# A list scheduler's second pass: urgencies taken from deadlines in a linear-attention and mixture-of-experts kernel

## The chip, the cores and the metric

The kernel runs on one core of a Trainium2 chip. The metric is the device time of one execution in microseconds (us), the median of several executions. Engines are named as the profile names them: PE is TensorE's matmul, PEld its weight load, DVE is VectorE, ACT is ScalarE, POOL is GpSimd, and SP is SyncE, which only issues DMAs here.

## The reference

Two stages follow each other. Linear attention: phi is applied to q and k, keys and values are summed into a small matrix for each head, and queries read it with a normalisation. Then four dense experts, each with two layers, weighted by given probabilities.

```python
def _attn_ref(q, k, v):                      # q, k, v: (8, 8, 576, 64)
    def phi(x):
        return np.where(x > 0, x, np.exp(x) - 1.0) + 1.0
    q_p, k_p = (phi(q), phi(k))
    kv = np.einsum('bhsd,bhse->bhde', k_p, v)
    z = np.sum(k_p, axis=2)
    num = np.einsum('bhsd,bhde->bhse', q_p, kv)
    den = np.einsum('bhsd,bhd->bhs', q_p, z)[..., None] + 1e-06
    return (num / den).astype(np.float32)

def _moe_ref(x, domain_probs, w1, w2):       # x: (4608, 512), 4 experts, 512 -> 1024 -> 512
    p = domain_probs / (domain_probs.sum(-1, keepdims=True) + 1e-09)
    for e in range(E):
        h = np.maximum(x @ w1[e], 0.0)
        out += p[:, e:e + 1] * (h @ w2[e])
```

## The kernel before

The kernel writes no order by hand. Every piece of work is an operation of a planner (class `Plan`): `pl.add` records its engine, an assumed duration, an urgency `pri` (smaller is earlier), the function that emits its instructions, and what it reads and writes. Dependencies follow from these names. A DMA also has `lead` and `move`, the time before and during its movement; all movements share one assumed mover, and landing takes another 0.6 us before time 80 and 2.5 us after. A result used on another engine comes 0.28 us later (`HOP`), on the same engine 0.03.

`Plan.order` then lays all operations out in time. At each step it takes the engine that can start something first and, among the operations ready there within 0.1 us (`NEAR`), the one with the smallest urgency. POOL is an exception: its operations keep the order in which they were recorded. The operations are emitted in the order of the starts found, and each engine executes its own in that order.

The work falls into three parts.

- Start, to about 84 us. Batch 0's attention is computed pair of heads by pair (`attention`, `turn_x`), its rest rows by `rest_maps` and `rest_late`. POOL loads the weights and most of the inputs of batches 0 and 1. Batch 0 goes through the experts in plain products (`first_l1`, lines L594 and L626; `first_l2`, L604 and L661), with batch 1's attention between them. DVE forms sums of weights (`sums_w1` L546, `sums_w2` L567).
- The main stage, 64 units (block of rows, half, expert). A unit's times hang on `U(n) = 84 + 6.4 n`. `prep` scales x by the probabilities on ACT (xp, L706, urgency U-7) and transposes it by DMA from SP (xT, L708, three buffers). `xsums` forms differences of xT on DVE (xs, L724). `l1_seven` has seven products of 8 matmuls on three PSUM banks (L746), each followed by an ACT copy or relu (L763, L760) or a DVE fused relu (L766). Product 5 and product 7 of a unit write the same bank, with the relu between them. `ssums` forms differences of the hidden values on DVE (s4, L808), and `l2_unit` the seven products of the second layer (L822), interleaved with the next unit's first layer. After every fourth unit DVE adds up the output (L893 to L900) and SP stores it. The last unit has its own ending (L861, L888), with two stores from SP and two from ACT.
- Beside the units runs the attention of batches 2 to 7, a pair for every two units, from a hand-set time t on: loads from SP (L232), exp on ACT (ek, L412, urgencies t and t+1.5), phi on DVE (kqp, L404 and L405, t+1.5 and t+3), the values cast on ACT (vp, L408), the query's transpose from SP (qT, L443, t+4.5; in the first two batches on PE, L424 and L437), the key-value product on PE (kv, L457 and L460, t+6), its copy (kvz, L470), two products (nd, L481, t+7.5 and t+9) and two normalisations on DVE (L495, L497, t+8.25 and t+9.75).

A first-layer product at step i of unit n has urgency U(n)+0.9i, a second-layer one U(n+1)+0.45+0.9i.

Of the kernel before, what the change touches and what calls it, by code (L numbers as in the profile page):

```python
# [17 lines left out]
BIG = 3.0e38  # L18


class Plan:
# [3 lines left out]

    HOP = 0.28
    NEAR = 0.1

    def __init__(self):
# [4 lines left out]
    def add(self, eng, dur, pri, fn, r=(), w=(), move=0.0, after=0.0, lead=1.2):  # L36
# [15 lines left out]
        )  # L52
        return n

    def order(self):
        ops = self.ops
        left = [len(o["deps"]) for o in ops]
        users = [[] for _ in ops]
        for n, o in enumerate(ops):
            for d in o["deps"]:  # L60
                users[d].append(n)
        free = {o["eng"]: 0.0 for o in ops}
        ready = {e: {} for e in free}
        fixed = {"POOL": [n for n, o in enumerate(ops) if o["eng"] == "POOL"]}
        at = [o["after"] for o in ops]
        mover = 0.0

        def release(n):
            ready[ops[n]["eng"]][n] = at[n]

        for n in range(len(ops)):
            if left[n] == 0:
                release(n)
        start = [0.0] * len(ops)
        for _ in ops:
            best = None
            for e, cand in ready.items():
                if e in fixed:
                    cand = {n: cand[n] for n in fixed[e][:1] if n in cand}
                if not cand:  # L80
                    continue
                t = max(free[e], min(cand.values()))
                if best is None or t < best[0]:
                    best = (t, e, cand)
            t, e, cand = best
            n = min(
                (n for n, x in cand.items() if x <= t + self.NEAR),
                key=lambda n: (ops[n]["pri"], n),
            )
            o = ops[n]  # L90
            del ready[e][n]
            if e in fixed:
                fixed[e].pop(0)
            start[n] = max(t, at[n])
            free[e] = done = start[n] + o["dur"]
            if o["move"]:
                mover = max(done + o["lead"], mover) + o["move"]
                done = mover + (0.6 if mover < 80 else 2.5)
            o["start"], o["done"] = start[n], done
            for u in users[n]:  # L100
                lat = self.HOP if ops[u]["eng"] != e or o["move"] else 0.03
                at[u] = max(at[u], done + lat)
                left[u] -= 1
                if left[u] == 0:
                    release(u)
        return [ops[n] for n in sorted(range(len(ops)), key=lambda n: (start[n], n))]
# [932 lines left out]
```

## Time and profile before

| | us |
|---|---|
| median of 7 executions | 502.12 |
| lowest and highest | 501.82 and 504.18 |
| the profiled execution, its own time | 502.12 |
| its span in the profile | 500.4 |
| PE busy | 481.4 |
| DVE busy | 410.1 |
| ACT busy | 368.1 |
| POOL busy | 42.6 |
| HBM read and written | 45.16 and 9.44 MB |

The span is what the profile covers; about 1.7 us of the execution's time lie around it. A busy share is an average over parts of the program with different limits, so the stretches of the span are read one by one: first the landing of loads and the first pairs, then batch 0 in the experts, then the units, then the end. The number after L in the profile is a line of the kernel above. A group's name such as `l1b<-xs,w` is the tile written and the tiles read.

### The profile page before, as it was taken

What the parts mean: (1) busy time and instruction counts of PE and PEld (TensorE: products, weight loads), DVE (VectorE), ACT (ScalarE), POOL (GpSimd) and SP (SyncE); (2) the same over time, 40 slices, a digit from 0 to 9 for tenths busy, and PEclk for the clock granted to TensorE, in tenths of its full rate; (3) what the DMA queues carried; (4) which work ended last, traced back from release to release, by engine and by line L of the source; (5) the groups of instructions that cost most, each with busy time, mean ns of one, the idle gap of its engine ahead of it and who ended that gap; (6) DMA issues with size and microseconds to landing.
All of it is one profiled execution on the core that took longest, in us unless ns stands there. A gap on an engine that the chain in (4) does not pass through costs nothing.

```text
span 500.4 us, 14836 instructions
## 1 busy us (share of the span) xinstructions
PE 481.4 (96%) x6008; PEld 424.2 (85%) x6008; DVE 410.1 (82%) x1036; ACT 368.1 (74%) x694; POOL 42.6 (9%) x68
## 2 busy tenths in 40 slices
PE   2799999999999999999999999999999999999995
PEld 1444546999999999999999999999999999999994
DVE  6788997889998999798998898899988676767664
ACT  5737667987987798869886888788866767676541
POOL 8856400000000000000000000000000000000000
PEclk9999999999999999999999999999999999999999
DMA  8999947935777577465467674757632232323311
GB/s 242 233 236 231 263 107 167 262 74 159 145 159 161 127 150 157 114 185 138 128 117 176 116 182 117 139 144 148 153 61 78 52 86 45 86 44 85 45 44 44
DMA packets 124006, 67.51 MB, mean 135 GB/s; under 512 B 94480, under 2 KB 117776, under 8 KB 123936
## 3 DMA queue, kind: packets, MB, share of 16 engines
q1 hardware_dynamic: 115056, 51.53, 45.7%
q0 software_dynamic: 8720, 14.76, 13.8%
q8 instruction: 47, 0.77, 0.6%
q10 hardware_dynamic: 160, 0.26, 0.1%
q14 instruction: 23, 0.19, 0.1%
HBM read 45.16 MB, written 9.44 MB: 109 GB/s over the span
## 4 chain that ended last, share of the span: by engine, by line
PE 90%; DMA 3%; ACT 2%; DVE 2%; issue 1%; POOL 1%; DVEq 0%; POOLq 0%; ACTq 0%
PE l1b L746 38%; PE l2b L822 38%; PE l2b L604 5%; PE l1b L594 5%; DMA w<-in_moe_w_dram 2%; PE at L481 2%; PE at L457 1%; DMA vs<-in_v_dram 1%; ACT xp L706 1%; DVE ot L661 1%; ACT h L760 0%; DVE ot L888 0%; POOL kq L232 0%; PE at L460 0%; ACT p L763 0%
## 5 line engine op out<-in xcount | busy, mean ns | idle before, releaser
L746 PEld LDWEIGHTS <-w 128*128 128x128 f16 x2048 | 132.5, 98 | 4.7
L760 ACT ACTIVATE h<-l1b 128x512 f16<-128x512 f32 x128 | 76.8, 600 | 53.8 <-PE l1b L746 52.2
L822 PE MATMUL l2b<-w,h 128*128 128x256 f16 x768 | 114.9, 273 | 0.1
L822 PE MATMUL l2b<-t,s 128*128 128x256 f16 x768 | 112.6, 273 | 0.0
L746 PEld LDWEIGHTS <-w1x 128*128 128x128 f16 x1536 | 100.0, 98 | 5.0 <-issue 1.5
L822 PEld LDWEIGHTS <-s 128*128 128x128 f16 x1024 | 92.3, 98 | 7.3
L766 DVE CUSTOM_DVE_ANT_0 h<-l1b,p 128x512 f16<-128x512 f32 x64 | 44.1, 690 | 44.9 <-PE l1b L746 40.5
L746 PE MATMUL l1b<-xs,w1x 128*128 128x128 f16 x1024 | 78.0, 219 | 0.5 <-ACT l1b L763 0.3
L746 PE MATMUL l1b<-xT,w 128*128 128x128 f16 x1024 | 78.1, 219 | 0.0
L746 PE MATMUL l1b<-xs,w 128*128 128x128 f16 x1024 | 78.0, 219 | 0.0
L706 ACT ACTIVATE xp<-x,p_nat 128x512 f16<-128x512 f16 x112 | 76.3, 720 | 1.4 <-DMA xT<-xp 0.6
L822 PEld LDWEIGHTS <-h 128*128 128x128 f16 x768 | 67.4, 98 | 5.1 <-ACT h L760 0.4
L808 DVE TENSOR_TENSOR s<-h 128x512 f16<-128x512 f16 x128 | 53.8, 420 | 1.4
L763 ACT COPY u<-l1b 128x512 f32<-128x512 f32 x64 | 37.5, 585 | 12.5 <-PE l1b L746 12.2
L766 DVE CUSTOM_DVE_ANT_0 h<-l1b,u 128x512 f16<-128x512 f32 x64 | 43.8, 684 | 3.5 <-PE l1b L746 2.2
L763 ACT COPY l1b<-l1b 128x512 f32<-128x512 f32 x64 | 36.6, 572 | 13.1 <-PE l1b L746 11.8
L763 ACT COPY p<-l1b 128x512 f32<-128x512 f32 x64 | 37.5, 585 | 8.8 <-PE l1b L746 7.6
L724 DVE TENSOR_TENSOR xs<-xT,xs 128x256 f16<-128x256 f16 x128 | 36.9, 288 | 4.1 <-PE l1b L746 0.5
L412 ACT ACTIVATE ek<-kq 128x512 f16<-128x512 f32 x60 | 37.8, 631 | 2.1 <-DMA kq<-in_k_dram 1.7
L746 PE MATMUL l1b<-xT,w1x 128*128 128x128 f16 x512 | 39.0, 219 | 0.1
L822 PE MATMUL l2b<-w,s 128*128 128x256 f16 x256 | 38.4, 273 | 0.0
L405 DVE TENSOR_TENSOR kqp<-ek,kqp 128x512 f16<-128x512 f16 x64 | 27.2, 425 | 10.0 <-ACT ek L412 6.5
(114 smaller groups left out, 562.3 us busy)
## 6 DMA issues: line engine op xcount, KB each, us to landing
w<-in_moe_w_dram POOLq DMA_DIRECT2D x32, 256.0 KB, 7.2
out_dram<-ot SPq DMA_DIRECT2D x16, 512.0 KB, 3.1
kq<-in_k_dram SPq DMA_DIRECT2D x25, 256.0 KB, 3.1
vs<-in_v_dram SPq DMA_DIRECT2D x25, 256.0 KB, 3.3
kq<-in_q_dram SPq DMA_DIRECT2D x25, 256.0 KB, 4.0
kq<-in_k_dram POOLq DMA_DIRECT2D x5, 256.0 KB, 8.1
vs<-in_v_dram POOLq DMA_DIRECT2D x5, 256.0 KB, 7.6
kq<-in_q_dram POOLq DMA_DIRECT2D x5, 256.0 KB, 7.0
```

Source lines behind the costliest of these rows:

```text
L405: nc.vector.tensor_tensor(out=o, in0=ek[:, i], in1=o, op=AO.min)
L412: pl.add("ACT", 0.55, pri + i * step, lambda i=i: nc.scalar.activation(ek[:, i], kq[:, i], AF.Exp), r=(sk[i],), w=(("ek", ei, i),))
L594: nc.tensor.matmul(out=bank, lhsT=w1_sb[e][:, dc, fj * P : (fj + 1) * P], rhs=xt0[:, dc, :], start=(dc == 0), stop=(dc == DC - 1),)
L604: nc.tensor.matmul(out=bank, lhsT=hts[ht[fj]][:, c * P : (c + 1) * P], rhs=w2_sb[e][:, fj, :], start=(fj == 0), stop=(fj == FC - 1),)
L706: pl.add("ACT", 0.6, pri, lambda c=c, src=src, ps=ps: nc.scalar.activation(xp[:, c, :], src, AF.Copy, scale=ps), r=r, w=(("xp", xi, c),))
L724: lambda o=o, a=a, b_=b_: tt(out=o, in0=a, in1=b_, op=AO.subtract),
L746: nc.tensor.matmul(out=bank[:, fc * P : (fc + 1) * P], lhsT=wt[:, kc, fc * P : (fc + 1) * P], rhs=r[:, kc, :], start=(start and fc == 0 an ...
L760: return lambda: nc.scalar.activation(o, bank, AF.Relu)
L763: return lambda: nc.scalar.copy(o, bank)
L766: return lambda: nc.vector._custom_dve(TENSOR_ADD_SAT, out=o, in0=bank, in1=t, s0=BIG, s1=0.0)
L808: pl.add("DVE", 0.36, U(n + 1) + d - 0.5, lambda i=i, a=a, b_=b_, alu=alu: tt(out=s4[:, i], in0=a, in1=b_, op=alu), r=r, w=(Q(i),))
L822: nc.tensor.matmul(out=l2b[bank][:, half * HD : (half + 1) * HD], lhsT=a[:, c, :], rhs=w[:, c], start=(opens and first and c == 0), stop=( ...
```

## The change

`order` is renamed to `lay_out`, and a new `order` runs it twice. Between the two passes `deadlines` goes backward through all operations. A PE operation's deadline is its start in the first pass; every other one's is the earliest of its users' deadlines, less the delay to that user and its own duration; for a DMA also less `lead`, `move` and a landing time of 0.6 us, whatever the time. An operation that no PE operation depends on keeps the value BIG. These deadlines replace the urgencies of all operations that are not on PE; those on PE keep the hand-set ones. The second pass starts afresh with them, and its order is emitted. The landing time in the layout itself is now written as LAND, with 1.9 us added from time 80 on.

```diff
     HOP = 0.28
+    LAND = 0.6
     NEAR = 0.1
...
+    def deadlines(self):
+        ops = self.ops
+        late = [o["start"] if o["eng"] == "PE" else BIG for o in ops]
+        for n in range(len(ops) - 1, -1, -1):
+            o = ops[n]
+            for d in o["deps"]:
+                x = ops[d]
+                lat = self.HOP if x["eng"] != o["eng"] or x["move"] else 0.03
+                if x["move"]:
+                    lat += x["lead"] + x["move"] + self.LAND
+                late[d] = min(late[d], late[n] - lat - x["dur"])
+        for n, o in enumerate(ops):
+            if o["eng"] != "PE":
+                o["pri"] = late[n]
+
     def order(self):
+        self.lay_out()
+        self.deadlines()
+        return self.lay_out()
+
+    def lay_out(self):
         ops = self.ops
         left = [len(o["deps"]) for o in ops]
...
             if o["move"]:
                 mover = max(done + o["lead"], mover) + o["move"]
-                done = mover + (0.6 if mover < 80 else 2.5)
+                done = mover + self.LAND + (0.0 if mover < 80 else 1.9)
```

## The prediction

> **What bounds the kernel now.** I read the busy table first, then the stretches, then TensorE's waits, then the timelines around the two places where a changed order could matter. The page gives the size of the prize:
>
> ```profile
> span 500.4 us, 14836 instructions
> PE 481.4 (96%) x6008; PEld 424.2 (85%) x6008; DVE 410.1 (82%) x1036; ACT 368.1 (74%) x694; POOL 42.6 (9%) x68
> ```
>
> TensorE is busy for 481.4 of 500.4 us, so at most 19 us are idle on it, and DVE and ACT have room. Where those 19 us lie decides everything, because the change only orders work. The stretches (us, then the busy time of each engine in them):
>
> ```profile
> 0.00:7.50 7.50, 0.00 (x0) 0.10 (x1) 4.39 (x17) 3.06 (x4) 6.52 (x15) 1.00 0.72 197
> 7.50:24.14 16.64, 11.96 (x81) 7.17 (x81) 11.96 (x35) 12.63 (x28) 14.06 (x22) 1.00 1.15 257
> 24.14:84.00 59.86, 58.98 (x333) 28.90 (x333) 51.02 (x111) 35.97 (x70) 21.97 (x33) 1.00 0.93 198
> 84.00:380.00 296.00, 295.60 (x4054) 279.56 (x4052) 264.03 (x688) 242.14 (x465) 0.00 (x0) 1.00 0.64 145
> 380.00:491.30 111.30, 111.30 (x1517) 105.62 (x1515) 74.61 (x180) 73.07 (x126) 0.00 (x0) 1.00 0.28 59
> 491.30:500.40 9.10, 3.51 (x33) 2.90 (x30) 4.12 (x10) 1.25 (x3) 0.00 (x0) 0.99 0.20 60
> ```
>
> The first PE column against the length of the stretch: idle 7.50, 4.68, 0.88, 0.40, 0.00 and 5.59 us. The main stage, 407 us with all 64 units of seven products, has 0.40 us of idle time in all. DVE is busy there for 264.03 of 296.00 us (89%) and ACT for 242.14 (82%). TensorE's waits, in total, times and longest:
>
> ```profile
> PE l2b L457 <- ACT vp L408: 7.9, 2, 7.5
> PE l2b L424 <- DVE kqp L405: 1.3, 2, 0.7
> PE l1b L594 <- ACT s L589: 1.1, 3, 0.6
> PE l2b L584 <- DVE x L497: 0.8, 3, 0.3
> PE at L481 <- ACT qT L437: 0.8, 2, 0.4
> PE l1b L594 <- DMA w<-in_moe_w_dram: 0.7, 1, 0.7
> PE l1b L746 <- ACT l1b L763: 0.3, 1, 0.3
> ```
>
> All but the last row belong to the attention of batches 0 and 1; the same answer for 84 us to the end is empty. The row that blames the weight load is doubtful, as these two lines of the ACT and PE timelines show:
>
> ```profile
> 23.50 0.59 ACT L589 COPY s<-l2b 128x512 f16<-128x512 f16 x1 [1.33 <-PE l2b L584]
> 24.14 0.81 PE L594 MATMUL l1b<-s,w 128*128 128x512 f16 x3 [0.67 <-DMA w<-in_moe_w_dram]
> ```
>
> The copy ends at 24.09, and the product follows 0.05 us later, as it does after the three earlier copies (15.26 to 15.31, 18.23 to 18.27, 22.16 to 22.21). So it is the chain of pair 3 of batch 0 that releases it: load, exp, phi, turn, qT, nd, norm, turn_x, copy.
>
> **The change part by part.** No instruction is added or removed; the second layout and the deadline loop run when the program is built. The split of 2.5 into LAND and 1.9 leaves the layout's sum at 2.5. TensorE's urgencies stay as written by hand; its order can differ only where an operand is ready at another moment. POOL's order is fixed and its urgencies are not read: the weight and stage loads of the start keep their sequence. All of these: 0 us. What moves is the order on DVE, ACT and SP.
>
> *How far it moves.* With TensorE at its hand-written times, deadlines can be worked out from the source. The fused relu after product 5 had U+4.5; its bank is written again by product 7 at U+5.4, less 0.28 and 0.62: U+4.5, unmoved. The four s4 differences had 1.5, 2.4, 3.3 and 3.9 after the next U; from the second-layer products at 2.25, 4.05, 4.95 and 5.85, less 0.64, they get 1.6, 3.4, 4.3 and 5.2. The phi of the keys goes from t+1.5 to t+6-0.28-0.92 = t+4.8; that of the queries stays (t+3.0 to t+3.1, through its transpose). The first normalisation goes from t+8.25 to t+9-0.28-0.74 = t+8.0. The scaled copies xp go from U-7 to U-0.28-2.3-1.25-0.28-0.6 = U-4.7. So the chain that feeds the products keeps its place or gains, and attention and xp mostly yield 1 to 3 us.
>
> *DVE in the main stage.* The tightest link is the fused relu between two products on one PSUM bank (DVE, then PE):
>
> ```profile
> 305.85 0.43 DVE L405 TENSOR_TENSOR kqp<-ek,kqp 128x512 f16<-128x512 f16 x1
> 306.54 0.69 DVE L766 CUSTOM_DVE_ANT_0 h<-l1b,p 128x512 f16<-128x512 f32 x1 [0.26 <-PE l1b L746]
> ...
> 305.79 0.61 PE L746 MATMUL l1b<-xs,w 128*128 128x128 f16 x8
> 307.55 0.61 PE L746 MATMUL l1b<-xs,w 128*128 128x128 f16 x8
> ```
>
> The relu ends at 307.23, the product that needs the bank starts at 307.55: 0.32 us to spare. A phi (L404 at 305.39 to the end of L405 at 306.28, 0.89 us) that DVE begins just before the relu's operand is there would push it by up to 0.89 and stop PE for 0.57. Queued behind it would be the s4 differences and the other relu, and behind the stopped product all of PE. There are 46 such phis after 84 us: from below 0 (before has nothing left to gain there, at most its 0.40), from above 46 x 0.57 = 26 us. I take one of them, 0.6 us, since the nearest row is that of before, with no such wait in 64 units, and the deadlines do not put phis ahead of relus.
>
> *ACT in the main stage.* The copy u of product 3 (304.67 to 305.26) has 0.53 us before its bank is written at 305.79. An exp of 0.63 us or an xp of 0.72 us in front costs at most 0.2; ACT is idle 18% of the time, so 0, and 0.2 per case if that cover goes.
>
> *SP.* It issues transposes, pair loads and stores in one order, and all three kinds get new urgencies; a load placed ahead of a transpose holds it for its issue of 0.47 to 0.58 us. Most of its time it waits for buffers (105.4 us in 34 waits of the xT transposes for L746). The cover is large:
>
> ```profile
> 307.62 1.23 SPq L708 DMA_TRANSPOSE xT<-xp  x1
> 316.75 0.42 DVE L724 TENSOR_TENSOR xs<-xT 128x512 f16<-128x512 f16 x1
> ```
>
> This transpose waits for the unit three ahead of its own to let go of the buffer (its last reader, the L724 at 307.14, ends at 307.42). By that count its own unit begins its products at 321.38 and its sums at 316.75; with 3.1 us from issue to landing it is there at 310.7, 6.0 us early. Stores without a later PE reader get the urgency BIG and go last; the output buffer is next written 8 units (52 us) later, so 0.
>
> Here a rule speaks against the change: the deadlines allow 0.6 us for landing where the layout, after 80 us, allows 2.5. From a transpose's issue they allow 1.25+0.2+1.5+0.6 = 3.55 us, and the trace has 3.1 (3.0 to 5.4). The Trainium skill, "DMA: Bandwidth & Descriptors", Anatomy of one DMA, puts a fixed cost of about 2.0 us on every DMA, mostly the receipt of the last write; it was measured on the POOL path, not SP's. Set in place of 0.6 it makes the deadlines 1.4 us too late, and the layout's own figure 1.9. By the trace the term is 0, by the rule 1.4 to 1.9 per transpose if nothing covered it. I take 0: even 1.9 is less than the 6.0 us of cover.
>
> *The first 84 us.* What pairs 0 to 3 do is bound by landings and by a chain of about ten steps; the first layout already starts nearly every PE step there when it is ready, so deadlines mostly repeat its order. One place could gain: exp q of pair 3 stood on ACT behind two copies (18.60 us, while DVE had begun the same phi at 17.34 and then waited 1.51 for it): 1.3 us. In the other direction one more misplaced copy costs its 0.6 us. I take 0, between -1.3 and +1.3. Of the 0.88 us from 24.14 to 84, 0.59 is PE waiting at 67.58 for a phi that stood behind a normalisation; half a chance of losing that wait: -0.3.
>
> The clock is a second place for a rule. The granted clock reads 1.00 in every stretch, but three products L594 with their successor take 1.23 us from 15.31 to 16.54 and 0.64 from 24.14 to 24.78: half speed before 19 us. "TensorE: Matmul & The Clock Gate", What's actually happening, says that the array starts at half rate and is released after some 3.4 us of sustained work. By it, denser early work would save up to 7 x 0.2 = 1.4 us; by the chain it saves nothing, since what follows waits for pair 3 and not for PE. I take 0 and put the 1.4 into the low end.
>
> *The end.* The last unit's order is set by readiness; last stores 495.46 and 496.1, nothing competes: 0.
>
> **Sum.** 0.6 - 0.3 + 0 = +0.3 us on a profiled execution of 502.12 us (span 500.4 and 1.7 around it), which is also the median of the runs: 502.4 us.
>
> **Rivals.**
>
> *Collisions in the main stage (slower).* The mechanism of the relu above, at L766: deadlines come from the planner's 0.62 and 0.92, while the trace has 0.69 and 0.89, and where before's hand-set offsets happened to leave no collision, nothing in the new order guards against them. For it: DVE at 89%, 0.32 us to spare. Against it: DVE stands idle in front of that relu in 24 cases from 100 to 400 us, 17.2 us. It decides from the second collision (2 x 0.57 = 1.1 us). With a quarter of 46 phis, 11 x 0.57 = 6.3 us: 508.4; with five, 505.0.
>
> *A worse start (slower).* Chain of pair 3, one or two ACT operations of 0.6 us or a phi of 0.89 misplaced: +1.2 to 1.8, 503.6. For it: the planner has these loads landing in a chain of 0.7 and 1.4 us moves, while POOL loads here take 5.9 to 6.5 us to land, so its idea of what is ready is off.
>
> *A better start (faster).* exp q moves up (-1.3) and the waits of the middle go (-0.6 of 0.88): 500.2; with half of the first alone, 501.2. Against it: that exp's place comes from when the planner thinks its load lands, which does not change.
>
> *The change does nothing visible* (order almost the same): 502.1, inside the likeliest case.
>
> **How the numbers follow.** A measurement of this kernel can tell about 0.2%, 1.0 us, from no change. Likeliest, within 1.0 us: 0.40, at 502.4 (its own range 501.2 to 503.1). Collisions 0.25, worse start 0.14, so slower 0.39; better start 0.21. The range reaches from 500.7, which leaves out half of the better start, to 507.5, which leaves out the worst of the collisions.
>
> **What would show it.** Right: PE idle from 84 to 491 us stays under 1 us, the waits of PE after 84 stay empty, the first L746 stays at 82.4 within 0.5, the tail at 9.1. Collisions: rows of L746 waiting for DVE h L766 (or ACT l1b and u L763). A late transpose: L746 or DVE xs waiting for DMA xT. Start: the copy L589 at 23.50 and the product at 24.14 move together. Many waits on PE beyond 100 us, or a first L746 before 81.4, would prove me wrong.

## The result: 1.7 us faster, about half of it from a wait that the planner does not see

| | before | after |
|---|---|---|
| median, us | 502.31 (37 runs) | 500.60 (15 runs) |
| lowest and highest, us | 501.36 and 504.19 | 500.21 and 501.30 |
| profiled execution: its time, its span, us | 502.12, 500.4 | 500.44, 498.6 |
| ratio of the runs to those of before, 95% interval | | 0.9966 [0.9958, 0.9975] |
| first product of the units (L746; after: L770) starts at, us | 82.43 | 81.67 |
| from there to the start of the last group of L822 (after: L846), us | 411.78 | 410.76 |

Line numbers of after are 24 higher than those of before. The end is unchanged: from the start of the last group to the end of the span it takes 6.2 us in both. So the 1.8 us between the spans are 0.76 before the first unit and 1.02 within the units.

The page of after, first lines (busy time and instructions):

```profile
span 498.6 us, 14821 instructions
PE 479.9 (96%) x6008; PEld 424.1 (85%) x6008; DVE 410.5 (82%) x1036; ACT 368.8 (74%) x694; POOL 42.6 (9%) x68
```

The same 6008 matmuls and the same work on DVE and ACT. PE's idle time went from 19.0 to 18.7 us, its busy time from 481.4 to 479.9. Five sixths of the gain are thus in what the page calls busy. The stretches of after, in the columns of before's (length, PE, PEld, DVE, ACT, POOL, clock, DMA share, GB/s):

```profile
7.50:24.14 16.64, 12.21 (x84) 7.29 (x83) 12.60 (x36) 12.79 (x29) 14.24 (x22) 1.00 1.14 258
24.14:84.00 59.86, 58.99 (x345) 29.41 (x344) 50.79 (x112) 36.59 (x72) 21.81 (x33) 1.00 0.96 200
84.00:380.00 296.00, 295.55 (x4066) 280.38 (x4064) 265.55 (x690) 242.64 (x465) 0.00 (x0) 1.00 0.64 144
```

From 84 to 380 us PE is 0.45 us idle, against 0.40 before: read this way, the units gained nothing. But 4066 matmul records lie in the stretch and not 4054. And TensorE's waits in after (who, for whom, total, times, longest):

```profile
PE l2b L481 <- DVE kqpr L347: 7.4, 1, 7.4
PE l1b L618 <- ACT s L613: 1.6, 3, 0.7
PE l2b L448 <- DVE kqp L429: 1.3, 2, 0.7
...
PE l1b L770 <- ACT l1b L787: 0.3, 1, 0.3
PE l1b L770 <- DVE xs L748: 0.3, 1, 0.3
```

Hardly a row is shorter. The row that blamed the weight load is gone; that product is now put down to its copy, as the earlier three were. These two lines, ACT then PE, answer to 23.50 and 24.14 of before:

```profile
22.73 0.59 ACT L613 COPY s<-l2b 128x512 f16<-128x512 f16 x1 [1.33 <-PE l2b L608]
23.37 0.81 PE L618 MATMUL l1b<-s,w 128*128 128x512 f16 x3 [0.67 <-ACT s L613]
```

The tight link between two products on one bank looks as it did. In after (DVE, PE) the relu ends at 305.25, and the product that needs its bank starts at 305.58: 0.33 us to spare, where before had 0.32:

```profile
304.56 0.69 DVE L790 CUSTOM_DVE_ANT_0 h<-l1b,p 128x512 f16<-128x512 f32 x1 [0.33 <-PE l1b L770]
305.58 0.61 PE L770 MATMUL l1b<-xs,w 128*128 128x128 f16 x8
```

**Where the start got its 0.76 us.** Up to 24 us PE, POOL and SP execute the same order in both, DVE's differs only from 21.9 us on, and ACT's by one exchange: the first copy kvz now stands behind the exp of the next pair. What changed more is one time. The first two lines are from the PE and ACT timelines of before, the third is from ACT's of after:

```profile
11.68 0.32 PE L481 MATMUL l2b<-kvz,qT 128*128 128x130 f16 x1
12.04 0.21 ACT L470 CAST kvz<-l2b 64x65 f16<-64x65 f32 x1 [0.70 <-PE l2b L481]
```

```profile
11.08 0.21 ACT L494 CAST kvz<-l2b 64x65 f16<-64x65 f32 x1
```

This is the copy of pair 1's key-value product. Its operand was ready at 10.95 in before (L460 at 10.63), yet it waited until 12.00 for a product of pair 0 that writes another part of the same PSUM bank (`l2b2n` beside `l2b2k`). The planner keeps the two parts apart. The framework that turns the emitted operations into instructions gave the copy a wait on everything emitted earlier on PE for that bank: in the program of before it waits for PE's 18th semaphore step, which this L481 gives, in after for the 14th, which is its own L484. The planner's first layout had the copy at 9.95 and the product at 9.92; the second has 9.71 and 9.91. So the order of emission turned over.

The lead can be followed from there to the product at 24.14 (23.37 in after), 0.77 us earlier. L594 works in chunks of four matmuls, one chunk for each pair of heads, and that product opens the fourth. After the copy ACT works on without a pause in before, up to the copy (14.68; in after 13.85) that releases the first chunk of the expert's first layer (15.31 and 14.65). By the start of the second chunk 0.53 us of lead are left (18.27 and 17.74). The rest comes while that chunk runs (PE of before, then of after):

```profile
18.27 1.09 PE L594 MATMUL l1b<-s,w 128*128 128x512 f16 x3 [0.25 <-ACT s L589]
19.20 0.38 PE L594 MATMUL l2b<-s,w 128*128 128x512 f16 x1
```

```profile
17.74 0.85 PE L618 MATMUL l1b<-s,w 128*128 128x512 f16 x3 [0.33 <-ACT s L613]
18.43 0.38 PE L618 MATMUL l2b<-s,w 128*128 128x512 f16 x1
```

Three matmuls took 0.93 us in before and 0.69 in after, since the half speed that the prediction describes lasted further into it in before: its matmuls follow each other after 0.38, 0.33 and 0.22 us, in after it is 0.26, 0.22 and 0.21. From their end to the fourth chunk it is 4.94 us in both. So in these two executions 0.24 of the 0.77 us belong to the half speed and not to the wait.

**Where the units got their 1.02 us.** The densest spacing in the trace is 0.0556 us for a matmul of 128 columns and 0.1092 for one of 256 (eight L746 start to next start 0.44 to 0.45, four L822 0.44). A place where the start that follows a product of the units comes more than 0.06 us later than that is a gap. Before has 14 of them after 82 us, about 2.4 us together; after has 7, 1.4 us. Most are shorter than the 0.16 us by which the modelled end of a matmul outlasts the next one's start, so no row of waits names them. Here is the longest in the middle of before (PE, then ACT):

```profile
180.09 1.33 PE L746 MATMUL l1b<-xs,w1x 128*128 128x128 f16 x16
...
178.31 0.71 ACT L706 ACTIVATE xp<-x,p_nat 128x512 f16<-128x512 f16 x1
179.56 0.60 ACT L760 ACTIVATE h<-l1b 128x512 f16<-128x512 f32 x1 [0.53 <-PE l1b L746]
180.19 0.57 ACT L763 COPY l1b<-l1b 128x512 f32<-128x512 f32 x1
```

Sixteen matmuls take 16 x 0.0556 + 0.16 = 1.05 us; these took 1.33, so 0.27 are lost in their midst, and the line says "busy". The second eight start at 180.81, when the copy that stands behind the relu on ACT has ended. Nothing foreign held ACT up here: it was idle for 0.53 us until the relu's product was done. TensorE ran two first-layer products on end, and the second had to wait for this copy. In after a second-layer product stands between the same two, and the gap is gone:

```profile
177.85 0.61 PE L770 MATMUL l1b<-xs,w1x 128*128 128x128 f16 x8
178.30 0.60 PE L846 MATMUL l2b<-w,h 128*128 128x256 f16 x4
178.74 0.61 PE L770 MATMUL l1b<-xs,w1x 128*128 128x128 f16 x8
```

TensorE's own order has thus changed, although its urgencies have not: the planner can start only a product whose operands are ready, and in the second pass these are ready at other times. Compared place by place, 1293 of the 6008 matmuls of the two profiles are not the same, the first of them at 85.5 us in after.

### The profile page after: what moved, and what is told of

It reads as the page before. It is cut to its first block, busy times and chain, and to the rows that moved or that the text cites. A ratio compares the mean times of both kernels' runs of the same rounds, so it can differ in the third digit from the quotient of the medians.

```text
span 498.6 us, 14821 instructions
## 1 busy us (share of the span) xinstructions
PE 479.9 (96%) x6008; PEld 424.1 (85%) x6008; DVE 410.5 (82%) x1036; ACT 368.8 (74%) x694; POOL 42.6 (9%) x68
## 4 chain that ended last, share of the span: by engine, by line
PE 89%; DVE 3%; ACT 3%; DMA 2%; POOL 1%; issue 1%; DVEq 0%; POOLq 0%; ACTq 0%
PE l1b L770 38%; PE l2b L846 37%; PE l1b L618 5%; PE l2b L628 5%; DMA vs<-in_v_dram 2%; PE at L505 2%; PE at L481 1%; DVE ot L685 1%; ACT xp L730 1%; DVE s L832 1%; DVE ot L912 0%; DVE h L790 0%; ACT ek L351 0%; ACT s L613 0%; ACT h L784 0%
## 5 line engine op out<-in xcount | busy, mean ns | idle before, releaser
L770 PEld LDWEIGHTS <-w 128*128 128x128 f16 x2048 | 133.3, 98 | 5.3 <-issue 0.2
L846 PE MATMUL l2b<-t,s 128*128 128x256 f16 x768 | 114.7, 273 | 0.0
L846 PE MATMUL l2b<-w,h 128*128 128x256 f16 x768 | 114.7, 273 | 0.0
L770 PEld LDWEIGHTS <-w1x 128*128 128x128 f16 x1536 | 100.3, 98 | 4.7 <-issue 0.9
L846 PEld LDWEIGHTS <-s 128*128 128x128 f16 x1024 | 90.7, 98 | 6.5
L770 PE MATMUL l1b<-xs,w1x 128*128 128x128 f16 x1024 | 78.0, 219 | 0.6 <-ACT l1b L787 0.3
L770 PE MATMUL l1b<-xT,w 128*128 128x128 f16 x1024 | 78.0, 219 | 0.1
L770 PE MATMUL l1b<-xs,w 128*128 128x128 f16 x1024 | 78.0, 219 | 0.0
L730 ACT ACTIVATE xp<-x,p_nat 128x512 f16<-128x512 f16 x112 | 77.3, 721 | 0.6 <-DVE x L521 0.2
L846 PEld LDWEIGHTS <-h 128*128 128x128 f16 x768 | 67.3, 98 | 4.6
L770 PE MATMUL l1b<-xT,w1x 128*128 128x128 f16 x512 | 39.0, 219 | 0.0
L846 PE MATMUL l2b<-w,s 128*128 128x256 f16 x256 | 38.4, 273 | 0.0
```

The source lines that it names most:

```text
L730: pl.add("ACT", 0.6, pri, lambda c=c, src=src, ps=ps: nc.scalar.activation(xp[:, c, :], src, AF.Copy, scale=ps), r=r, w=(("xp", xi, c),))
L770: nc.tensor.matmul(out=bank[:, fc * P : (fc + 1) * P], lhsT=wt[:, kc, fc * P : (fc + 1) * P], rhs=r[:, kc, :], start=(start and fc == 0 an ...
L846: nc.tensor.matmul(out=l2b[bank][:, half * HD : (half + 1) * HD], lhsT=a[:, c, :], rhs=w[:, c], start=(opens and first and c == 0), stop=( ...
```

## The experiments

All times come with the ratio to before, run on the same chip, and its interval. Before's median was 502.94 us beside experiments 1 to 4, 502.41 beside 5 to 8 and 502.29 beside 9 to 12, so the ratios are to be compared and not the times. "Stretch" is the time from the first product of the units to the start of the last group, 411.78 us before; three kernels whose units keep hand-set urgencies have 411.78, 411.98 and 411.96, mean 411.91.

**1. Before, with one copy emitted earlier**

```diff
+        at_ = list(start)
+        n = [n for n, o in enumerate(ops) if o["w"] == (("kvz", 1),) and o["eng"] == "ACT"][0]
+        at_[n] -= 0.25
-        return [ops[n] for n in sorted(range(len(ops)), key=lambda n: (start[n], n))]
+        return [ops[n] for n in sorted(range(len(ops)), key=lambda n: (at_[n], n))]
```

> The kernel before, with one operation emitted 0.25 us earlier in the program's order: the copy kvz of pair 1, batch 0. Each engine's own order stays that of before; what changes is that the copy is now emitted ahead of the second product nd of pair 0, which writes another part of the same PSUM bank, so its wait on PE counts to the last L460 of its own pair and no longer to that L481. Theory A (the 0.77 us gained before 24 us come from this wait): ACT L470 starts at 11.1 to 11.2 us and no longer at 12.04, the fourth chunk of L594 at 23.3 to 23.5 and no longer at 24.14, time 501.5 us or 0.6 to 0.8 below before. Theory B (they come from the exchange of the first kvz copy with the next exp on ACT): no change, 502.2 us, the fourth chunk at 24.1.

Measured: 501.98 us, 0.9980 [0.9972, 0.9988], so 0.6 to 1.4 us below before. Stretch 411.98. The ACT and PE timelines of this kernel:

```profile
11.29 0.21 ACT L473 CAST kvz<-l2b 64x65 f16<-64x65 f32 x1
23.87 0.81 PE L597 MATMUL l1b<-s,w 128*128 128x512 f16 x3 [0.67 <-ACT s L592]
```

The copy is at 11.29 and without a wait. The fourth chunk, at 23.87, came 0.3 earlier than before in this one execution, not the 0.6 to 0.8 expected; over 22 runs the time moved as Theory A said. One exchange in the order of emission, with no engine's own order touched, is worth about 1 us by the medians. Before's 75 runs here scatter from 501.30 to 504.65 us, these 22 from 501.25 to 502.60, and no profile shows why; at the lower quarter of the runs the gain is 0.5 us (501.80 against 502.26), close to the 0.53 us that the two profiles have ahead of the second chunk. That the exchange gains is shown; whether 0.5 or 1 us is not.

**2. After, with the same copy emitted later**

The same edit with `+= 0.25`, in after.

> The kernel after, with the copy kvz of pair 1 emitted 0.25 us later, behind the second product nd of pair 0; each engine's own order stays that of after. Theory A: the wait is back, the fourth chunk of L594 (there L618) at 24.0 to 24.2 us, and the time 0.6 to 0.8 above after, 1.0 below before: 501.3 us. Theory B: as after, 500.6 us.

Measured: 501.97 us, 0.9982 [0.9974, 0.9991]. After's interval ends at 0.9975, so they hardly overlap; stretch 410.82, as in after.

```profile
12.18 0.21 ACT L497 CAST kvz<-l2b 64x65 f16<-64x65 f32 x1 [0.71 <-PE l2b L508]
24.80 0.81 PE L621 MATMUL l1b<-s,w 128*128 128x512 f16 x3 [0.67 <-ACT s L616]
```

The wait is back, the chunk is late, the gain of the start is gone and that of the units stays. The exchange of kvz with exp, which this kernel keeps, brings nothing by itself: Theory B falls. What it did was to move the second copy in the planner's layout, and so to turn the emission over.

**3 and 4. Deadlines for one part of the time alone**

```diff
-            if o["eng"] != "PE":
+            if o["eng"] != "PE" and o["start"] >= 60:    # 3; in 4: < 60
                 o["pri"] = late[n]
```

> The change with deadlines only for operations whose start in the first pass is 60 us or later; the others keep their hand-set urgencies. If gains of the start and of the units are separate and add up, this has the units' part alone: 1.0 us below before (501.2 us), with the fourth chunk at 24.1 as before and fewer short gaps between products after 82 us. If the units' gain is only a consequence of their earlier start, 0.

> The change with deadlines only for operations whose start in the first pass is below 60 us. Adding up: 0.8 us below before (501.5 us), fourth chunk at 23.4, gaps after 82 us as in before. If the whole gain hangs on the start, 1.7 below before (500.6 us).

Measured: units alone 501.52 us, 0.9974 [0.9965, 0.9984], stretch 410.79. Start alone 501.97 us, 0.9981 [0.9972, 0.9990], stretch 411.96. Their product is 0.9955, and after measured 0.9966 [0.9958, 0.9975] on another occasion: within what the intervals allow, the parts are separate and add up.

The fourth chunk in 3 was expected at 24.1 and came at 23.71, though its copy waits (11.89). So I read the start over all the single profiles. The first unit starts at 82.43, 83.10, 82.04, 82.90, 82.80, 82.22, 81.96 and 82.68 us in the eight kernels with the wait (mean 82.52), and at 81.67, 82.17, 82.04, 81.90, 81.65 and 81.71 in the six without (mean 81.86). The difference of 0.66 us is clear of the scatter of the means, but one execution alone scatters by as much. Of it 0.50 us are there when the second chunk starts (mean 18.35 and 17.85). From that start to the fourth chunk it takes 5.58 us in the six profiles in which the chunk's three matmuls take 0.64 or 0.65 us, and up to 6.39 (experiment 2) where the half speed reaches into it; with the wait and without it both kinds occur.

**5, 6 and 7. Deadlines in the units for one engine alone**

```diff
-            if o["eng"] != "PE":
+            if o["eng"] == "DVE" and o["start"] >= 60:    # 6: "ACT"; 7: "SP"
                 o["pri"] = late[n]
```

> The change with deadlines only for VectorE's operations that start at 60 us or later in the first pass; ACT, SP and the start keep hand-set urgencies. The stretch from the first product L770 to the start of the last group of L846 was 411.8 to 412.0 us with hand-set urgencies and 410.8 with deadlines. Theory A (the short gaps are relus and differences standing behind attention on VectorE): 410.8 to 411.0 and a time 0.9 us below before, 501.9 to 502.0. Theory B (ACT's copies between products): 411.8. Theory C (SP's transposes): 411.8.

> The same for ScalarE's operations alone. Theory A: stretch 411.8, time as before. Theory B: 410.8 to 411.0, time 0.9 us below before. Theory C: 411.8.

> The same for the operations that SP issues alone. Theories A and B: 411.8, time as before, since transposes land some 6 us ahead of use. Theory C: 410.8 to 411.0 and a time 0.9 us below before.

| deadlines for | stretch, us | against 411.91 | time, us | ratio |
|---|---|---|---|---|
| DVE | 410.95 | -0.96 | 501.55 | 0.9978 [0.9966, 0.9989] |
| ACT | 411.28 | -0.63 | 501.83 | 0.9990 [0.9979, 1.0000] |
| SP | 410.57 | -1.34 | 501.58 | 0.9974 [0.9960, 0.9987] |
| all three (after) | 410.76 | -1.15 | | |

None of the three theories holds as stated: by the stretch of one profile each, every set alone brings more than half of the gain, SP's the most, and the three sum to 2.93 where all together bring 1.15. In the time, ACT's is not clear of zero. The sets do not isolate an engine, though: new urgencies for one engine change when everything else is ready, so the second pass lays out all engines anew. Against before, TensorE's order differs in 1294, 970 and 987 places (DVE, ACT, SP), and in none where the deadlines stop at 60 us (experiment 4). So no engine's order is shown to be at fault, and TensorE's own may be the one that counts; no run here holds it fixed. What the profiles show is about a dozen short gaps, partly in other places in each layout. After has such places too, and its longest is new (ACT, then PE):

```profile
332.57 1.33 ACT L730 ACTIVATE xp<-x,p_nat 128x512 f16<-128x512 f16 x2
333.81 0.57 ACT L784 ACTIVATE h<-l1b 128x512 f16<-128x512 f32 x1
334.42 0.57 ACT L787 COPY l1b<-l1b 128x512 f32<-128x512 f32 x1
...
334.11 0.60 PE L846 MATMUL l2b<-t,s 128*128 128x256 f16 x4
335.04 0.61 PE L770 MATMUL l1b<-xs,w1x 128*128 128x128 f16 x8 [0.33 <-ACT l1b L787]
```

Two copies xp (1.33 us) hold up a relu and the copy behind it. Four L846 should take 0.44 us and the next product starts 0.93 after their start, 0.49 lost.

**8. After, with all four copies kvz of batch 0 emitted earlier**

```diff
+            if o["eng"] == "ACT" and o["w"] and o["w"][0][0] == "kvz" and start[n] < 25:
+                at_[n] -= 0.25
```

> The kernel after, with the four copies kvz of batch 0 emitted 0.25 us earlier in the program's order. The copy of pair 2 then no longer waits for the normalisation of pair 1 (L521, ends at 15.39 us), but for its own product, ready at about 14.9. If that wait is on the chain of the start, 0.3 to 0.6 us below after: 500.1 us, ratio to before 0.996. If PE is the limit there (the fused chunk of L618 from 14.65 to 16.36 stands ahead of the next turn), as after: ratio 0.9966. More than 0.2 us above after would say that the order of emission matters in another way.

Measured: 500.76 us, 0.9967 [0.9954, 0.9980]: as after. The copy of pair 2 moved from 15.48 to 14.89 and nothing followed from it, since the next turn of PE stands behind the first chunk (L618 of after, here L622, 14.71 to 16.37). Not every wait of this kind costs; pair 1's was on the chain, pair 2's was not.

**9 and 10. No deadlines, random moves of the hand-set urgencies**

```diff
+        rnd = random.Random(1)    # 10: 2
         for n, o in enumerate(ops):
-            if o["eng"] != "PE":
-                o["pri"] = late[n]
+            if o["eng"] != "PE" and o["start"] >= 60:
+                o["pri"] += rnd.uniform(-0.5, 0.5)
```

> Hand-set urgencies throughout, but those of all operations off PE that start at 60 us or later in the first pass are moved by a random amount between -0.5 and +0.5 us (seed 1); no deadlines at all. Three single-engine sets of deadlines had each shortened the stretch of the units (411.8 to 412.0 us with hand-set urgencies) to 410.6 to 411.3, so the question is whether deadlines carry information or whether any other order would do. Theory D (deadlines carry it): 411.7 us or more, since random moves only make new collisions; time as before or up to 1 us above. Theory E (the hand-set order was an unlucky draw, and any reshuffling is as good): 410.6 to 411.3 us, time 0.6 to 1.2 below before.

> The same with another draw (seed 2). Theory D: 411.7 us or more. Theory E: 410.6 to 411.3 us. One of each would mean that single orders scatter by as much as the effect itself.

Measured: 502.48 us, 0.9997 [0.9987, 1.0007], stretch 411.97; and 502.20 us, 0.9992 [0.9981, 1.0004], stretch 411.42. The first is what Theory D says, the second lies between. Reshuffling alone is worth 0 to 0.5 us in these two draws; the four sets of the table brought 0.6 to 1.3. That all four gain, and one of two draws does not, speaks for Theory D, but ACT's 0.63 and the second draw's 0.49 are close: how much of the 1.15 us is luck of the draw, two draws cannot say. TensorE's order differs from before's in 1085 and 970 places in them too, so a changed order there is not enough for a gain.

**11. Deadlines with the layout's own landing time**

```diff
                     lat += x["lead"] + x["move"] + self.LAND
+                    lat += 0.0 if x["start"] < 80 else 1.9
```

> The change with deadlines that allow for a DMA's landing what the layout allows, 2.5 us from time 80 on in place of 0.6. If transposes were placed too late by the short allowance, this gains on after; the cover of some 6 us found in the trace of before says no: stretch of the units 410.6 to 410.9, time as after within 0.4 us, ratio to before 0.9966.

Measured: 500.41 us, 0.9956 [0.9940, 0.9972], stretch 410.78 against 410.76. The short allowance costs nothing that can be measured, as the cover of 6 us in the profile of before had said.

**12. Deadlines for all at the start, for SP alone in the units**

```diff
-            if o["eng"] != "PE":
+            if o["eng"] != "PE" and (o["start"] < 60 or o["eng"] == "SP"):
                 o["pri"] = late[n]
```

> A candidate for a better version: deadlines for all engines below 60 us, and from there on for SP alone, the set with the shortest stretch so far (410.57 us against 410.76 with all). If the two parts add up: copy kvz of batch 0's pair 1 without its wait as in after, stretch 410.5 to 410.7, time 0.1 to 0.3 below after, 500.4 us.

Measured: 500.33 us, 0.9954 [0.9939, 0.9970], stretch 410.45, gaps about 1.0 us. It has the lowest median and the shortest stretch of all, but its interval overlaps after's, and experiment 11, run beside it with deadlines for all, has 500.41: that it beats after is not shown.

## Why the prediction was wrong

I forecast 502.4 us, "within 1.0 us: 0.40", with 0.21 for faster. It became 500.6, 0.1 below the range. Point by point:

- *"before has nothing left to gain there, at most its 0.40"*: this step failed. It took PE's idle column for the time that could be lost, and that column hides gaps shorter than the modelled tail of a matmul (0.16 us at each place). By starts there were about 2.4 us to gain, of which 1.0 were gained. My term was +0.6; it measured -1.0. It is the larger error, 1.6 of the 2.0 us between the sum and the result. The sign I named for being right, under 1 us of idle time on PE from 84 to 491 us, came true (0.45) and could not see this.
- *"deadlines mostly repeat its order ... I take 0, between -1.3 and +1.3"* for the first 84 us: the order on the engines was indeed repeated, up to one exchange. That this makes the time the same was the wrong conclusion. The order in which operations of different engines are emitted also changed, and with it which instruction a wait counts to. Measured in its place: -0.76 in the profiles (0.53 before the second chunk, the rest half speed), -0.6 to -1.4 in experiment 1. I named as the only place to gain the exp of pair 3 behind two copies (18.60); in after it is still behind the same two (18.07). That my rival of a better start, at 500.2 to 501.2, takes in the result is luck: neither of its two gains came. Its 501.2 is a slip as well; half of 1.3 below 502.1 is 501.5.
- *"-0.3"* for the wait at 67.58: it did not go. After has it at 66.81, again 0.59 us, for the same phi.
- *Collisions at the fused relu*: the mechanism exists, the place was wrong. The relu kept its 0.33 us to spare in the unit shown. What the product waits for in the gaps shown, in both kernels, is ACT's copy, which I had put at "0, and 0.2 per case"; in after, at 334.11, it costs 0.49.
- *The change's worked-out shifts* (attention and xp yield 1 to 3 us, the chain of products keeps its place) fit the outcome, but no run here tests them one by one. TensorE's order, which I let differ "only where an operand is ready at another moment" and put at 0, differs in 1293 places, and at 180 us that removes a gap of 0.27.
- *LAND, the clock term, the end*: 0 each. Experiment 11 bears out the first and the profiles the last. The clock term had its reason wrong ("what follows waits for pair 3 and not for PE"): the second chunk lies on the chain, and its half speed cost 0.3 us in before and none in experiment 4 (0.93 and 0.65 us). Whether the change of order moves its end, or chance does, stays open (last section).

## What to carry to other kernels

When PE is "busy" throughout, count its starts against the densest spacing in the trace before you say that nothing is left; here idle columns and rows of waits began only where a modelled tail of 0.16 us ended. In a kernel whose order comes from a planner, the order of emission across engines is an order too: where two regions share a bank that the framework treats as one, a pair of operations that turns over by 0.03 us can add or remove a wait of 0.7. And when three parts of a change bring, one by one, more than the whole, check first that each of them moves only what it names: here each laid out every engine anew.

## What was not expected of the hardware

TensorE's half speed at the start ended at another moment from execution to execution. The second chunk of the expert's first layer (three matmuls up to the start of the fourth, begun between 17.7 and 18.4 us) took 0.69 us in after, 0.93 in before, 0.65 in experiment 4 and 1.23 in experiment 2, while the granted clock reads 1.00 in all. The Trainium skill, "TensorE: Matmul & The Clock Gate", What's actually happening, says that the window over which the array's activity is watched runs freely, so that the point of release varies; these four times agree with that, and no run here isolates it. It is a part of why single profiles of the start scatter by more than half a microsecond.

The planner's own layouts put the stretch of the units at 415.6 us with hand-set urgencies and 413.4 with deadlines, a gain of 2.2 where the chip gave 1.0, and they rank the single engines DVE, ACT, SP (1.5, 0.8, 0.5), where the chip has SP, DVE, ACT (1.3, 1.0, 0.6). Its sign was right for all of these, its ranking was not.
